# Attention and mixture of experts in one kernel: output writes issued by two engines in turn, more constant products, the last expert's first products in halves, its last casts split three to five

## The chip, the cores and the metric

The kernel runs on one core of a Trainium2 chip, as a single launch. The metric is the device time of one execution in microseconds. The value before is the median of three runs. A fourth execution was taken by the hardware profiler, and all views below are of that one.

## The reference

Two stages follow each other. The first is attention for 4 batches, 8 heads, 768 positions and head width 64. Three heads are causal over all earlier keys; the other five keep only the last 64 keys and 4 "sink" keys. The second is a mixture of 8 experts with early exit, over the 3072 rows of 512 columns that attention makes.

```python
scores = scale * q @ k.T                      # per batch and head
mask = causal if retrieval_head else causal & (is_sink | in_window)
x = softmax(where(mask, scores, -1e9)) @ v    # -> [3072, 512]

out = x.copy()
take = x @ w_skip > 0                         # the other rows leave as they are
e = argmax(x[take] @ w_gate); g = its softmax weight
out[take] = x[take] + g * (relu(x[take] @ w1[e]) @ w2[e])
```

Activations are 0.1-scaled normal draws; the weights are 8 x 512 x 1024 twice, in fp32, 33.5 MB in all.

## The kernel before

Every piece of work is an entry of a planner (`Plan`): a name, an engine, an assumed duration, what it depends on, and a key (the lowest goes first among those ready). The planner lays the entries out in time once, at build, and writes the instructions in the order of their planned starts; `manual_schedule` keeps that order. So an assumed duration or a key that is changed in one place can reorder instructions elsewhere, on every engine. On the chip each engine runs its own list in order and waits at semaphores. The DMAs are planned as well, on a common queue `Q`.

**Attention.** Sixteen pairs of heads, i = 0 to 15, four per batch. SyncE (SP) issues the loads of Q, K and V in fp32 (`load_qk`, `load_v`), four pairs ahead. GpSimd (POOL) casts them (`Cq`, `Ck`, `Cv`), TensorE (PE) transposes them (`Tq`, `Tk`, `Tv`), ScalarE (ACT) and VectorE (DVE) copy them out of PSUM (`Oq`, `Ok`, `Ov`). Then PE makes transposed scores in chunks of 1024 columns (`E`, L852 and L864), ACT takes their exponential (`X`, L874), PE weighs V with them (`PV`, L919), and DVE divides (`Nr`, `Nl`, `Nx`, L938 to L955) into the SBUF tile `x` of the batch. The chunks use two PSUM tiles `pst` in turn, so a chunk of scores waits for the exponential two chunks back.

**Writes of x.** When a batch's last pair is divided, `x_out` writes the batch to the output in HBM in two halves (`xo`, L976, 768 KB each). For the last batch it is four pieces: columns 0 to 255 after pair 13, 256 to 383 after pair 14, and two halves of the rest, which ACT divides itself (`n_last`, L969). All ten writes stand in SP's list, among the loads.

**Routing and gathers.** The gate logits come out of the same products (extra columns of V). DVE turns them into expert, rank and slot (`r`), PE into an index table, and `idx` (L1225) ends it. From there POOL gathers rows of x by index from HBM, 16 tiles of 128 rows, two per expert (`G`, L1259), and writes the results back by index (`S`, L1272).

**Experts.** For expert e and tile t: `cx` casts the gathered rows (DVE, L1286), `tx` transposes them (PE, L1295), `ox` copies them out (DVE, L1306), `F(e, f2)` is a quarter of the first products (PE, 8 matmuls of 256 columns, L1315), `Re` its relu (ACT, L1326), `Y(t)` the second products (PE, L1337), `A` the scaled addition (DVE, L1343), `S` the write. `warm` (L1480) puts matmuls of constants on PE while the index is made and the first gathers are under way; nothing reads their result.

**Weights.** POOL issues the weights of experts 0 to 6 as DMAs that cast fp32 to fp16 (`W`, L478). They begin in the middle of attention and stand in POOL's list between its casts, gathers and writes. Weights of the last expert come as fp32 through SP (`load_last`, `V`, L1378) into the room of older weights. The first piece goes where expert 6's first weights lie, so it waits for `F(6, 3)`. DVE and ACT cast each piece to fp16, one half of the columns each (`cast_last`, L1385).

**Completion counters.** In the program as built, plain DMAs of SP and ACT take turns over eight completion counters. A DMA that takes a counter waits on its engine until the former user of that counter has landed.

Of the kernel before, what the change touches and what calls it, by code (L numbers as in the profile page):

```python
# [8 lines left out]
FP32 = mybir.dt.float32  # L9
# [6 lines left out]
ACT = mybir.ActivationFunctionType  # L16
# [11 lines left out]
DM = H * D  # L28
E = 8
F = 1024  # L30
# [3 lines left out]
P = 128  # L34

DS = DM // P
FS = F // P
CAP = 256
# [14 lines left out]
class Plan:  # L53
# [9 lines left out]
    def op(self, name, eng, dur, fn, deps=(), key=0.0, lat=None, take=None,  # L63
           fill=None):


        o = dict(name=name, eng=eng, dur=dur, fn=fn, deps=list(deps), key=key,
                 lat=self.LAT if lat is None else lat, take=take, fill=fill,
                 seq=len(self.ops))
        self.ops.append(o)  # L70
        self.by[name] = o
        return name

    def dma(self, name, eng, issue, took, fn, deps=(), key=0.0, first=False,
            lat=1.9, fill=None):
        self.op((name, "go"), eng, issue, fn, deps, key, fill=fill)
        self.op(name, "Q", took, None, [(name, "go")], 0 if first else 1,
                lat=lat)
# [310 lines left out]
def kernel(  # L389
# [14 lines left out]
    nc = tc.nc  # L404
# [10 lines left out]
    Ov = out.rearrange("(b n p) d -> b p n d", b=B, p=P)  # L415
# [69 lines left out]
    with tc.tile_pool(name="sm", bufs=1) as sm_pool, \  # L485
# [3 lines left out]
        def pool(name, stack=pools, **kw):  # L489
# [17 lines left out]
        qk32, v32, c16, qTs, vTs, ats, psts, tps, xsb, lgh, opss = (  # L507
            {} for _ in range(11))
# [3 lines left out]
        op, dma = pl.op, pl.dma  # L512
# [145 lines left out]
        for i in range(NPR):  # L658
            for w in "qk":
                act = i == 0 and w == "k"  # L660
# [7 lines left out]
            elif i % 4 == 3 and i // 4 + 1 < B:  # L668
                b = i // 4 + 1
# [138 lines left out]
        for i in range(NPR):  # L808
# [7 lines left out]
            for hi in range(2):  # L816
# [10 lines left out]
               take=("tps", ("Ow", i)))  # L827
# [142 lines left out]
                                      opss[i][:, hi, c:c + D], recs[:, i, hi, n])  # L970
            return go

        def x_out(b, u, c0=0, c1=DM):
            def go():
                n = slice(0, NQB) if u is None else slice(3 * u, 3 * u + 3)
                nc.sync.dma_start(out=Ov[b][:, n, c0:c1],  # L976
                                  in_=xsb[b][:, n, c0:c1])
            return go

# [11 lines left out]
        for i in range(NPR):  # L991
            b = i // 4
# [15 lines left out]
            if i % 4 == 3:  # L1008
                op(("Gs", b), "DVE", 0.61, g_sum(b), [("Nl", i)], k0 + 1.15,
                   take=("tps", ("r", 1, "oh")) if b == B - 1 else None)  # L1010


        for b in range(B - 1):
            for u in range(2):
                dma(("xo", b, u), "SP", 0.45, 2.05, x_out(b, u),
                    [("Nx", 4 * b + 3)], next(sp) - 1000)
        for i, u, c0, c1, took in ((13, None, 0, 256, 2.2), (14, None, 256, 384, 1.3),
                                   (15, 0, 384, 512, 0.65), (15, 1, 384, 512, 0.65)):
            dma(("xo", 3, i, u), "SP", 0.45, took, x_out(3, u, c0, c1),
                [("Nx", i) if u is None else ("Nx", i, u)], next(sp) - 1000)  # L1020


# [153 lines left out]
        for ph, c0, n, k0, last in ((0, 0, 18, 140, ("Gs", 2)),  # L1176
# [36 lines left out]
            if ph:  # L1213
# [6 lines left out]
               take=("tps", "idx") if ph == 0 else None)  # L1220
# [12 lines left out]
        M = Consts()  # L1233
# [17 lines left out]
        xTs, x16s, xtps, hts, hpss, ypss = ({} for _ in range(6))  # L1251
# [54 lines left out]
                nc.vector.tensor_copy(xTs[e][:, :, s2 * P:(s2 + 1) * P], xtps[t])  # L1306
            return go

        def first(e, f2):
            def go():  # L1310
                w1 = wts[e, 0].rearrange("p (s f j) -> p s j f", s=DS, j=FS)
                hps = M.hps.tile([P, 2, CAP], FP32, tag="hps", name="hps")
                for fi in range(2):
                    for s in range(DS):
                        nc.tensor.matmul(  # L1315
                            hps[:, fi, :], w1[:, s, 2 * f2 + fi], xTs[e][:, s, :],
                            start=(fi == 0 and s == 0),
                            stop=(fi == 1 and s == DS - 1))
                hpss[e, f2] = hps
            return go  # L1320

        def relu(e, f2):
# [45 lines left out]
        def load_last(n, u, c0, c1):  # L1368
            def go():
                at = STAGE[n, u]  # L1370
                if n in IN_V and u == 0:
                    wtile(n, ldv_pool, tag="vf", bufs=2)
                if c0 == 0:
                    kw = dict(tag="vf", bufs=2) if at in IN_V else dict(tag=f"w_{at}")
                    w32[n, u] = (ldv_pool if at in IN_V else wpool if at < NPRE else M.w).tile(
                        [P, 2 * CW], FP32, name=f"w32_{n}_{u}", **kw)
                c = 2 * u * CW
                nc.sync.dma_start(out=w32[n, u][:, c0:c1],  # L1378
                                  in_=(w1r, w2r)[n % 2][E - 1][:, c + c0:c + c1])
            return go  # L1380

        def cast_last(n, u, c0, c1, dve):
            def go():
                to = wts[E - 1, n % 2][:, 2 * u * CW + c0:2 * u * CW + c1]
                (nc.vector.tensor_copy if dve else nc.scalar.copy)(  # L1385
                    to, w32[n, u][:, c0:c1])
            return go
# [3 lines left out]
        V_of = {14: [], 15: []}  # L1391
        for n in (14, 15):
            for u in range(2):
                e, half = divmod(STAGE[n, u], 2)
                parts = 2 if (n, u) == (15, 1) else 1
                for m in range(parts):
                    c0, c1 = (2 * CW * x // parts for x in (m, m + 1))
                    dma(("V", n, u, m), "SP", 0.45, 2.6 / parts, load_last(n, u, c0, c1),
                        [(prev, "go"),
                         *((("Y", t, 1) for t in (2 * e, 2 * e + 1)) if half else [("F", e, 3)]),  # L1400
                         *(place[n] if n in place else [])], 0, fill=3.0)
                    prev = ("V", n, u, m)
                    for dve in range(2):
                        d0, d1 = (c0 + (c1 - c0) * x // 2 for x in (dve, dve + 1))
                        op(("W", n, u, m, dve), "DVE" if dve else "ACT", 0.95 / parts,
                           cast_last(n, u, d0, d1, dve), [("V", n, u, m)], 650 + u)
                        V_of[n].append((u, ("W", n, u, m, dve)))
        op("drain", "POOL", 4.6, lambda: nc.gpsimd.drain(), [("W", 13, 0), ("G", NT - 1)], 455)
        for t in range(NT):
            op(("cx", t), "DVE", 0.62, cast_x(t), [("G", t), ("tx", t - 2)], 600 + t)  # L1410
            op(("tx", t), "PE", 0.25, turn_x(t),
               [("cx", t), ("ox", t - 2), ("F", 0, 3) if t > 1 else None],
               600 + 10 * (t // 2) - 15, take=("tps", ("ox", t)))
            op(("ox", t), "DVE", 0.42, out_x(t),
               [("tx", t), ("F", t // 2 - 2, 3)], 600 + t)
        for e in range(E):
            for f2 in range(FS // 2):
                op(("F", e, f2), "PE", 0.88, first(e, f2),
                   [("ox", 2 * e + 1), ("W", 2 * e, 0), ("W", 2 * e, 1),
                    *(x for _, x in V_of.get(2 * e, ())),  # L1420
                    ("Re", e - 1, f2)],
                   600 + 10 * e)
                op(("Re", e, f2), "ACT", 0.62, relu(e, f2),
                   [("F", e, f2), ("Y", 2 * e - 3, 1)], 600 + 10 * e)
            for s2 in range(NSM):
                t = e * NSM + s2

                cuts = (0, 4, 6, 8) if e == E - 1 else (0, 4, 8)
                for x, (j0, j1) in enumerate(zip(cuts, cuts[1:])):
                    end_ = j1 == FS  # L1430
                    op(("Y", t, 1) if end_ else ("Y", t, 0, x), "PE", 0.218 * (j1 - j0),
                       second(t, j0, j1),
                       [("Re", e, (j1 - 1) // 2), ("W", 2 * e + 1, 0),
                        ("W", 2 * e + 1, j0 // 4),
                        *(y for u, y in V_of.get(2 * e + 1, ())
                          if u == j0 // 4 and (u == 0 or y[3] == (j0 - 4) // 2)),
                        ("Y", t, 0, x - 1) if x else None,
                        ("A", t - 2)], 600 + 10 * e + 15 + (x if e == E - 1 else s2))
                op(("A", t), "DVE", 0.75, add(t), [("Y", t, 1), "idx"], 598.5 + t)
                dma(("S", t), "POOL", 1.0, 0.4, scatter(t), [("A", t)], 450 + t, first=True)  # L1440
# [43 lines left out]

        for part, (m, after) in enumerate(((3, [("PV", NPR - 1, 1)]),
                                           (1, [("r", 0, "slots"), "swap"]),
                                           (6, [("r", 1, "slots"), "swap"]))):
            for n in range(m):
                op(("warm", part, n), "PE", 0.85, warm(part),
                   after + ([("warm", part, n - 1)] if n else []), 0)  # L1490
# [43 lines left out]
```

## Time and profile before

| | before |
|---|---|
| median of 3 runs | 194.55 us (194.17 to 194.61) |
| profiled execution | 191.98 us, of which the span of instructions is 190.4 us |
| busy in the span | PE 157.8 us, POOL 125.3, DVE 115.6, ACT 103.8 |
| mean granted TensorE clock | 0.959 of full |
| HBM read and written | 56.64 MB and 10.49 MB, 353 GB/s over the span |
| loads, plain writes (DMA ring of SP) | 28.97 MB, 45.7% of 16 engines over the span |
| casting weight loads, gathers, scatters (POOL) | 19.45 MB as written, 47.0% |
| DMA ring of ACT | 0.41 MB, 0.9% |

A row of the profile gives a source line, an engine, an operation and its tiles. SPq and POOLq are the instruction sequencers of SP and POOL. The DMA share of a stretch of time is the busy time of packets over 16 engines; over 1.00 more than one packet per engine was in flight. In casting loads only the fp16 bytes are counted.

### The profile page before, as it was taken

Reading aid. Unit: us, or ns where it says so; the run is one execution under the profiler, and the core shown is the slowest. Engines: PE = TensorE matmul, PEld = TensorE weight load, DVE = VectorE, ACT = ScalarE, POOL = GpSimd, SP = SyncE. Lnnn points to the kernel's source line nnn. Section 1 sums busy time; section 2 is a strip of 40 time slices with the busy share of each in tenths; the row PEclk is TensorE's granted clock in tenths of the full one; section 3 lists DMA queues with packets and bytes.
Section 4 is the critical chain, followed back from the end, with each engine's and each line's share of the span. In section 5 each row is a group of like instructions: output and inputs, shape, how many; then the busy total and the mean of one; then the engine's idle time right before and its main releaser. Section 6 shows DMA issues by size and latency. Waiting matters only on the chain.

```text
span 190.4 us, 4704 instructions
## 1 busy us (share of the span) xinstructions
PE 157.8 (83%) x1859; PEld 121.7 (64%) x1874; DVE 115.6 (61%) x249; ACT 103.8 (55%) x136; POOL 125.3 (66%) x211
## 2 busy tenths in 40 slices
PE   0596689998999999999966959699999996995930
PEld 0365678777888888788843428389678673734610
DVE  6738675969797888799988241565673433152320
ACT  2187329986799979989739903136133150423700
POOL 7545997699898999998588488887735234016040
PEclk9999969999999999999999997999999999998795
DMA  5999999988997999999999989999999999899510
GB/s 151 323 312 365 335 362 354 282 288 311 310 356 247 351 284 275 211 216 293 272 237 308 197 159 198 269 258 227 195 236 233 215 261 269 186 406 314 192 65 13
DMA packets 28384, 49.21 MB, mean 258 GB/s; under 512 B 5172, under 2 KB 21428, under 8 KB 27202
## 3 DMA queue, kind: packets, MB, share of 16 engines
q0 software_dynamic: 5728, 19.45, 47.0%
q1 hardware_dynamic: 21296, 28.97, 45.7%
q10 hardware_dynamic: 1330, 0.41, 0.9%
q8 instruction: 16, 0.26, 0.5%
q14 instruction: 14, 0.11, 0.2%
HBM read 56.64 MB, written 10.49 MB: 353 GB/s over the span
## 4 chain that ended last, share of the span: by engine, by line
PE 46%; DMA 18%; issue 13%; DVE 10%; POOL 6%; ACT 4%; POOLq 0%; ACTq 0%; DVEq 0%
PE pst L864 13%; DMA w<-in_moe_w_dram 8%; PE opsa L919 8%; DMA xg<-out_dram,idx 6%; PE pst L852 6%; PE hps L1315 6%; PE yps L1337 5%; PE tps L714 5%; POOL out_dram L1272 3%; DVE k L748 3%; ACT at L874 3%; DMA qf<-in_q_dram 2%; PE tps L725 2%; DMA out_dram<-x 2%; DVE vT L768 1%
## 5 line engine op out<-in xcount | busy, mean ns | idle before, releaser
L874 ACT ACTIVATE at<-pst 128x1024 f16<-128x1024 f32 (+1 forms) x60 | 58.3, 1013 | 14.7 <-PE pst L864 13.8
L1326 ACT ACTIVATE ht<-hps 128x512 f16<-128x512 f32 x32 | 19.1, 597 | 41.4 <-PE hps L1315 30.6
L1272 POOL DMA_INDIRECT out_dram<-xg,idx x16 | 16.6, 1034 | 33.4 <-DVE xg L1343 30.1
L864 PE MATMUL pst<-qT,k 128*128 128x128 f16 (+2 forms) x308 | 36.4, 239 | 2.4 <-ACT qT L740 0.9
L1315 PE MATMUL hps<-xT,w 128*128 128x256 f16 x256 | 33.0, 290 | 4.5 <-ACT w L1385 2.2
L1315 PEld LDWEIGHTS <-w 128*128 128x128 f16 x256 | 29.9, 147 | 7.9 <-ACT w L1385 2.9
L748 DVE COPY k<-tps 64x768 f16<-64x768 f16 x32 | 30.4, 951 | 6.3 <-PE tps L714 5.9
L864 PEld LDWEIGHTS <-k 128*128 128x128 f16 x308 | 24.7, 100 | 11.3 <-issue 2.6
L1337 PE MATMUL yps<-w,ht 128*128 128x512 f16 x128 | 29.1, 379 | 0.0
L1343 DVE SCALAR_TENSOR_TENSOR xg<-yps,gsl,xg 128x512 f32<-128x512 f32 x16 | 11.9, 749 | 16.8 <-PE yps L1337 16.7
L1259 POOL DMA_INDIRECT xg<-out_dram,idx x16 | 17.3, 1078 | 7.1 <-issue 3.7
L919 PE MATMUL opsa<-va,at 128*128 128x74 f16 x392 | 20.2, 199 | 1.5 <-DVE x L955 1.5
L1337 PEld LDWEIGHTS <-ht 128*128 128x128 f16 x128 | 12.2, 98 | 13.0
L919 PEld LDWEIGHTS <-at 128*128 128x128 f16 x472 | 18.6, 99 | 2.0 <-DVE x L955 1.8
L740 ACT COPY qT<-tps 128x768 f16<-128x768 f16 x16 | 12.8, 800 | 7.2 <-PE tps L714 7.2
L852 PE MATMUL pst<-smask,identb 128*128 128x512 bf16 (+3 forms) x49 | 16.2, 344 | 0.3 <-ACT at L874 0.2
L1286 DVE CAST x<-xg 128x512 f16<-128x512 f32 x16 | 10.0, 646 | 10.0 <-issue 5.6
L695 POOL CAST va<-vf 128x768 f16<-128x768 f32 x16 | 13.3, 830 | 2.2 <-PE opsa L919 1.1
L955 DVE TENSOR_TENSOR x<-opsa,recs 128x768 f32<-128x768 f32 x15 | 14.2, 945 | 0.0
L714 PE MATMUL tps<-ident,q 128*128 128x128 f16 x96 | 8.3, 224 | 7.1 <-DVE q L689 6.1
L759 POOL COPY kx<-k 64x256 f16<-64x256 f16 x20 | 8.0, 399 | 8.1 <-DVE k L748 7.4
L1306 DVE COPY xT<-xtp 128x512 f16<-128x512 f16 x16 | 6.3, 421 | 11.5 <-PE xtp L1295 11.2
(139 smaller groups left out, 254.6 us busy)
## 6 DMA issues: line engine op xcount, KB each, us to landing
w<-in_moe_w_dram POOLq DMA_DIRECT2D x16, 512.0 KB, 8.0
qf<-in_q_dram SPq DMA_DIRECT2D x16, 384.0 KB, 6.5
w<-in_moe_w_dram POOLq DMA_DIRECT2D x6, 1024.0 KB, 11.1
kf<-in_k_dram SPq DMA_DIRECT2D x15, 384.0 KB, 6.0
out_dram<-x SPq DMA_DIRECT2D x7, 768.0 KB, 9.4
w<-in_moe_w_dram SPq DMA_DIRECT2D x3, 1024.0 KB, 7.9
w<-in_moe_w_dram SPq DMA_DIRECT2D x2, 512.0 KB, 13.8
kf<-in_k_dram ACTq DMA_DIRECT2D x1, 384.0 KB, 4.8
```

The costliest lines, as they stand in the source:

```text
L714: nc.tensor.matmul(t[:, n], c16[w, i][:, n].rearrange("p h d -> p (h d)"), C.ident, is_transpose=True, start=(n == 0), stop=(n == NQB - 1))
L748: nc.vector.tensor_copy(to, ti)
L852: nc.tensor.matmul(pst[:, c0 - c * CH:c0 - c * CH + m].rearrange("p (n c) -> p n c", c=P), identb, mv, start=(n == 0), stop=(n == last))
L864: nc.tensor.matmul(pst[:, c0 - c * CH:c0 - c * CH + m * P], lt, qTs[i][:, qb * P:(qb + m) * P], start=(n == 0), stop=(n == last))
L874: nc.scalar.activation(ats[i][:, c * CH:c * CH + cn], psts[i, c][:, :cn], ACT.Exp, scale=SCALE)
L919: nc.tensor.matmul(opss[i][:, hi, qb * VA:(qb + 1) * VA], ats[i][:, b0 + c:b0 + c + P], vb, start=(n == 0), stop=(n == len(todo) - 1))
L955: nc.vector.tensor_mul(xsb[i // 4][:, :, h0 * D:(h0 + 2) * D].rearrange("p n (h d) -> p h n d", h=2), summed(i, GX, 512 - GX, D), recs[:, ...
L1259: h = nc.gpsimd.indirect_dma_start(out=M.xgs[:, t], out_offset=None, in_=out[:, :], in_offset=bass.IndirectOffsetOnAxis(ap=idx[:, t:t + 1] ...
L1272: h = nc.gpsimd.indirect_dma_start(out=out[:, :], out_offset=bass.IndirectOffsetOnAxis(ap=idx[:, t:t + 1], axis=0), in_=M.xgs[:, t], in_of ...
L1315: nc.tensor.matmul(hps[:, fi, :], w1[:, s, 2 * f2 + fi], xTs[e][:, s, :], start=(fi == 0 and s == 0), stop=(fi == 1 and s == DS - 1))
L1326: nc.scalar.activation(hts[e][:, 2 * f2:2 * f2 + 2], hpss[e, f2], ACT.Relu)
L1337: nc.tensor.matmul(ypss[t], hts[e][:, j, s2 * P:(s2 + 1) * P], w2[:, j], start=(j == 0), stop=(j == FS - 1))
```

## The change

1. Writes of x alternate between SP and ACT: the second half of each of batches 0 to 2, the piece of pair 14 and the last half piece go to ACT's list.
2. Two more entries of constant products of four matmuls each stand ahead of the first expert (32 matmuls in place of 24).
3. For expert 7 each `F` is cut in two: the lower half of the contraction, which needs only the first piece of the weights, and the upper half. All four PSUM tiles are held open between.
4. The casts of the last expert are cut at three eighths: ACT casts 3/8 of the columns and DVE 5/8.
5. The key of `tx` is raised from -15 to -9, behind the first products of the expert before it.

```diff
-        def x_out(b, u, c0=0, c1=DM):
+        def x_out(b, u, c0=0, c1=DM, act=False):
...
-                nc.sync.dma_start(out=Ov[b][:, n, c0:c1],
+                (nc.scalar if act else nc.sync).dma_start(out=Ov[b][:, n, c0:c1],
                                   in_=xsb[b][:, n, c0:c1])
...
         for b in range(B - 1):
             for u in range(2):
-                dma(("xo", b, u), "SP", 0.45, 2.05, x_out(b, u),
+                dma(("xo", b, u), "ACT" if u else "SP", 0.45, 2.05, x_out(b, u, act=u == 1),
                     [("Nx", 4 * b + 3)], next(sp) - 1000)
...
-            dma(("xo", 3, i, u), "SP", 0.45, took, x_out(3, u, c0, c1),
+            act = i == 14 or u == 1
+            dma(("xo", 3, i, u), "ACT" if act else "SP", 0.45, took, x_out(3, u, c0, c1, act),
...
-        def first(e, f2):
+        def first(e, f2, s0=0, s1=DS):
...
-                    for s in range(DS):
+                    for s in range(s0, s1):
...
-                        d0, d1 = (c0 + (c1 - c0) * x // 2 for x in (dve, dve + 1))
-                        op(("W", n, u, m, dve), "DVE" if dve else "ACT", 0.95 / parts,
+                        cm = c0 + (c1 - c0) * 3 // 8
+                        d0, d1 = (cm, c1) if dve else (c0, cm)
+                        op(("W", n, u, m, dve), "DVE" if dve else "ACT", 0.85 / parts,
...
-               600 + 10 * (t // 2) - 15, take=("tps", ("ox", t)))
+               600 + 10 * (t // 2) - 9, take=("tps", ("ox", t)))
...
-                op(("F", e, f2), "PE", 0.88, first(e, f2),
+                two = e == E - 1
+                if two:
+                    op(("F", e, f2, 0), "PE", 0.44, first(e, f2, 0, DS // 2),
+                       [("ox", 2 * e + 1), ("W", 2 * e, 0),
+                        *(x for u, x in V_of.get(2 * e, ()) if u == 0),
+                        ("Re", e - 1, f2)],
+                       600 + 10 * e - 1)
+                op(("F", e, f2), "PE", 0.44 if two else 0.88,
+                   first(e, f2, DS // 2 if two else 0),
                    [("ox", 2 * e + 1), ("W", 2 * e, 0), ("W", 2 * e, 1),
                     *(x for _, x in V_of.get(2 * e, ())),
-                    ("Re", e - 1, f2)],
+                    ("F", e, f2, 0), ("Re", e - 1, f2)],
...
-                                           (6, [("r", 1, "slots"), "swap"]))):
+                                           (8, [("r", 1, "slots"), "swap"]))):
```

More of the change, by code (lines that the diff above doesn't have):

```diff
@@ L1307, in out_x @@
             return go
-        def first(e, f2):
+        def first(e, f2, s0=0, s1=DS):
             def go():
                 w1 = wts[e, 0].rearrange("p (s f j) -> p s j f", s=DS, j=FS)
-                hps = M.hps.tile([P, 2, CAP], FP32, tag="hps", name="hps")
+                if s0 == 0:
+                    hpss[e, f2] = M.hps.tile([P, 2, CAP], FP32, tag="hps", name="hps")
                 for fi in range(2):
-                    for s in range(DS):
+                    for s in range(s0, s1):
                         nc.tensor.matmul(
-                            hps[:, fi, :], w1[:, s, 2 * f2 + fi], xTs[e][:, s, :],
+                            hpss[e, f2][:, fi, :], w1[:, s, 2 * f2 + fi], xTs[e][:, s, :],
                             start=(fi == 0 and s == 0),
                             stop=(fi == 1 and s == DS - 1))
-                hpss[e, f2] = hps
             return go
```

## The prediction

> **What bounds the kernel now.** I began with the page's shares, its slices of DMA and clock, and the end of the chain.
>
> ```profile
> PE 46%; DMA 18%; issue 13%; DVE 10%; POOL 6%; ACT 4%; POOLq 0%; ACTq 0%; DVEq 0%
> DMA  5999999988997999999999989999999999899510
> PEclk9999969999999999999999997999999999998795
> ```
> ```profile
> 145.91 14.66 DMA w<-in_moe_w_dram
> 160.62 3.71 PE hps L1315 x32
> 164.33 5.19 PE yps L1337 x24
> ```
>
> TensorE leads the shares, but the late chain is a 14.66 us wait for w12 (the last weight load of expert 6, the twelfth of the late ones), landing at 160.62; F(6), by which I mean its quarters F(6, 0) to F(6, 3), the release of its buffers and the last expert follow. The DMA digits stay at 8 or 9 for two thirds of the span. In windows of 10 us the share is 1.01 or more from 60 to 105 us and from 120 to 160 us, so **the transfers set when the last experts start**. Where idle DMA time is left decides what a lost microsecond costs.
>
> ```profile
> 46.00:48.00 2.00, 1.32 (x21) 1.11 (x20) 1.93 (x5) 0.30 (x1) 1.94 (x6) 1.00 1.03 368
> 48.00:50.00 2.00, 1.95 (x36) 1.72 (x35) 1.97 (x3) 1.92 (x3) 1.84 (x5) 1.00 1.00 263
> 50.00:52.00 2.00, 2.00 (x42) 1.73 (x39) 1.02 (x3) 1.33 (x2) 1.85 (x4) 1.00 1.01 331
> 58.00:60.00 2.00, 2.00 (x38) 1.79 (x36) 1.70 (x2) 2.00 (x3) 1.28 (x4) 1.00 0.42 94
> 110.00:115.00 5.00, 2.69 (x18) 1.58 (x17) 1.95 (x4) 0.00 (x0) 4.08 (x5) 0.83 0.88 187
> 115.00:120.00 5.00, 5.00 (x37) 4.13 (x36) 1.42 (x3) 2.39 (x4) 3.99 (x5) 0.83 0.90 174
> ```
>
> The columns are stretch, length, busy PE, PEld, DVE, ACT and POOL, clock, DMA share, GB/s. After 46 us only two places have slack: 58 to 60 (1.16 us idle) and 110 to 120 (0.6 + 0.5 = 1.1 us).
>
> SyncE's timeline and DMA issues (KB, us to landing) show the first x writes, and its waits one thing more:
>
> ```profile
> 44.44 0.92 SPq L976 DMA_DIRECT2D out_dram<-x  x2
> 45.45 1.02 SPq L643 DMA_DIRECT2D kf<-in_k_dram  x1
> 46.57 1.89 SPq L643 DMA_DIRECT2D qf<-in_q_dram  x1
> 50.91 7.45 SPq L643 DMA_DIRECT2D qf<-in_q_dram  x1
> ```
> ```profile
> out_dram<-x SPq DMA_DIRECT2D x1, 768.0 KB, 6.8
> ```
> ```profile
> SPq L653 <- DMA kf<-in_k_dram: 1.4, 1, 1.4
> ```
>
> The second half of x, issued at 44.88, lands 6.8 us later at 51.7; the K load of pair 11 is issued right behind it, so no gap opens between them. The last line is a V load that waits for a K load it does not use: it takes over that load's completion counter.
>
> The tail, from the timeline:
>
> ```profile
> 171.48 0.44 PE L1315 MATMUL hps<-xT,w 128*128 128x256 f16 x2 [0.25 <-ACT w L1385]
> 173.86 5.16 PE L1315 MATMUL hps<-xT,w 128*128 128x256 f16 x30 [1.94 <-ACT w L1385]
> 178.86 3.62 PE L1337 MATMUL yps<-w,ht 128*128 128x512 f16 x16
> 180.35 0.62 ACT L1385 CAST w<-w 128x512 f16<-128x512 f32 x1 [0.19 <-DMA w<-in_moe_w_dram]
> 182.08 1.41 DVE L1343 SCALAR_TENSOR_TENSOR xg<-yps,gsl,xg 128x512 f32<-128x512 f32 x2 [1.30 <-PE yps L1337]
> ```
> ```profile
> 176.00:178.00 2.00, 2.00 (x11) 1.55 (x10) 0.69 (x1) 1.53 (x2) 0.00 (x0) 0.50 1.01 389
> ```
>
> TensorE waits 1.94 us inside F(7), then runs at half clock; the last weights land at about 180.3.
>
> **What the Trainium skill says.** "DMA: Bandwidth & Descriptors", section "Issuing engines are not separate DMA queues", says that issuing from several engines saves only sequencer time. The trace agrees: one ring alone shows shares of 1.0 and more. The same page, section "Latency and other measured facts", gives about 2 us of fixed cost, most of it the receipt of the write, and some 0.6 us to the first byte. Here x data start 0.9 us after issue, and the receipt takes about 1.4 us (data end about 50.3, landing 51.7). "TensorE: Matmul & The Clock Gate", section "Part 1: The HAM clock gate (the \"warmup\" mystery)", says that the clock halves after an idle window of about 3.4 us on a free-running grid. Here 0.50 came at 113.3 and 174.8, after gaps of only 1.7 and 1.9 us; a short gap can suffice.
>
> **Part 1: x writes on ScalarE.** The bytes are the same. Saved on SyncE: five issues of 0.37 to 0.49 us, worth nothing, since SyncE is not the limit. Added on ScalarE: five issues, taken at 0.5 (its K load took 0.50). Batch 0: ScalarE idles 1.72 us before 47.70; hidden. Batch 1: at 64.0, gap of 1.23 before 67.81; hidden. Batch 2: at 83.3, no gap; with the qT copy now ahead of it one exp comes 1.1 to 1.25 later, at most 0.4 us of TensorE stall, hidden while transfers lag. Batch 3: idle at 95.8 to 98.9 covers one, the other delays the zeros by 0.45, which have over 4 us; the routing before G0 ends at 107.3 and the last x lands at 104.8, so that stays covered.
>
> **The hidden wait.** Plain DMAs of SyncE and ScalarE share eight completion counters in turn. In the program as built, batch 0's second half takes counter 0 on ScalarE, and SyncE's K load of pair 11 is now the next user of counter 0: SyncE must wait until the write has landed. Before, that load's counter came from a load long finished. So the load is issued not at 45.45 but at about 51.75; its data start at 51.75 + 0.9 = 52.7. The x data end at about 50.3, behind them SyncE's other loads queue too, and GpSimd's first weight load comes only at 62.08. **DMA then stands idle for 52.7 - 50.3 = 2.4 us** (bounds 1.6 to 3.0, for an earlier receipt or a later first byte). The loads themselves have slack: pair 11's K would land at 55 for a cast at 57.34, the later Q and V 6 us or more ahead of theirs. But the bytes move back by 2.4 us. The idle 58 to 60 does not take this up: the Q load at 50.91 is held for 7.45 us in its issue, behind the big V load, until that has drained, so this gap moves along. From 60 on there is no slack until 110 to 120, where at most 1.1 is taken up; I take 0.7 (0.3 to 1.3), as part of that idleness is itself a wait for buffers. w12, F(6) and the last expert's loads: +2.4 - 0.7 = **+1.7 us**.
>
> **Part 2: eight more constant products.** 24 took 5.34 us from 105.5, 0.222 each: +1.78 ends them at 112.6, where the first transpose began at 112.52; cost 0.1 at most. F(0) ran at half clock (5.00 us for 32 products against 3.66 elsewhere), so 1.3 could be saved, but TensorE then waits in any case for the gather landing at 121.94: worth 0.
>
> **Part 3: moved transposes and w11.** Transposes go behind F(e-1), w11's issue behind S4 (about 144 instead of 139.1). w10 before it occupies the transfers to about 147.5, so this costs 0; if that cover fell, w11 would be late by up to 2 us before S5.
>
> **Part 4: halves and casts in the last expert.** Sixteen products fill the 1.94 wait; sixteen are left from about 173.7, at 0.115 each done at 175.5 if the clock stays full. Casts per column: VectorE 0.51 ns + 0.17 us, ScalarE 0.84 ns + 0.18 us (from 1024 and 512 columns: 0.69 and 0.43; 1.04 and 0.61). So 1280 and 768 columns take 0.82 and 0.83, against 0.69 and 1.04. Y then starts near 177.1, but its last pieces wait for weights landing at 180.3: the last cast ends 0.1 to 0.2 earlier, and the first accumulation at about 181.45 instead of 182.08 (less Y left behind it): -0.63 at most. Without a half clock before, only 0.1 is left. I take **-0.4** (0.1 to 0.7).
>
> **Sum.** +2.4 - 0.7 - 0.4 = +1.3 us against the profiled execution: 190.4 of span, 191.98 in all. The median of the runs, 194.55, lies 2.6 above that execution; I apply the difference to it: 195.85, say **195.8**. This case alone reaches from 195.2 to 197.0 (smallest and largest hole with the bounds above, not all at once).
>
> **Rivals.** *Stream end unmoved, faster (0.22).* The hole opens, but the stream is later held by buffers, not bytes: then slack at 110 to 120 and prefetch take it all, and the tail's -0.4 to -0.7 remains: 193.9. For it: the shares there lie below 1. Against it: only 1.1 us of slack is visible against 2.4. It decides if w12's landing moves by less than 0.1. *Half carried, no change (0.18).* A hole of 1.6 with 1.1 absorbed gives +0.5 against -0.4: 194.6. The delayed exp of batch 2, with no hole, ends there too. *The change does not do what it says:* the built order shows five of ten x writes on ScalarE, 32 constant products, F(7) as 16 and 16 products, casts of 768 and 1280 columns; excluded.
>
> **How the numbers follow.** Slower 0.60, same 0.18, faster 0.22; 0.3% (0.58 us) is about what a measurement of this kernel can tell from no change. The likeliest case sets 195.8; the range goes down to 193.8 for the others and up to 197.0.
>
> **What would show it.** After: SyncE waiting some 6 us on a DMA of x, its K load at 51 to 52, DMA share falling between 50 and 53; w12 landing 1 to 2 us later against the start; TensorE at full clock in 113 to 117 and 174 to 178; casts of 0.82; a shorter way from the last weights' landing to the first accumulation. I am wrong if the share shows no dip, or if there is a dip and w12 lands when it did.

## The result and the profile after

The changed kernel takes 199.4 us (median of 4 runs, 198.42 to 202.74) against 194.58 us before: 4.8 us or 2.5% more. Compared by the fast runs alone, those within 1.5% of their kernel's fastest, the ratio is 1.041 with a 95% interval of 1.033 to 1.050. The forecast had the side right and the size wrong: 195.8, with a range up to 197.0. The profiled execution after took 202.74 us, the slowest of its four runs and 3.3 above their median, where that of before lay 2.6 below its own; the two profiles therefore differ by more than the medians do, and places rather than totals are read from them.

The page after, clock and DMA in 40 slices:

```profile
PEclk9999999999999999975799999999999999699995
DMA  5999999799499999999699699999999999969901
```

There is a 4 among the DMA digits about a quarter of the way in, which was not there before, and the clock falls in slices 18 to 20, from about 86 to 101 us, where attention ran at full clock before.

The DMA queue of SyncE, its timeline and one of its waits:

```profile
43.27 0.39 SPq L976 DMA_DIRECT2D out_dram<-x  x1
53.85 0.37 SPq L643 DMA_DIRECT2D kf<-in_k_dram  x1
...
56.27 6.73 SPq L643 DMA_DIRECT2D qf<-in_q_dram  x1
...
67.15 0.52 SPq L643 DMA_DIRECT2D qf<-in_q_dram  x1
```
```profile
SPq L643 <- DMA out_dram<-x: 10.1, 1, 10.1
```

The K load that followed the x writes at 45.45 now goes out at 53.85. SyncE waited 10.1 us for an x write, the one that ScalarE issued at 43.28: in the trace's records that write and this K load count on the same semaphore, number 100, and the write landed at 53.79. In windows (columns as before) the transfers stop; the first three lines are those of before, the rest those after:

```profile
52.00:54.00 2.00, 1.93 (x32) 1.59 (x29) 1.57 (x4) 1.55 (x2) 1.49 (x3) 1.00 1.07 392
54.00:56.00 2.00, 1.95 (x41) 1.76 (x41) 1.90 (x4) 2.00 (x4) 1.85 (x4) 1.00 1.15 349
82.00:92.00 10.00, 9.90 (x176) 8.72 (x175) 9.66 (x22) 8.51 (x11) 8.20 (x19) 1.00 1.05 273
...
50.00:52.00 2.00, 2.00 (x36) 1.75 (x33) 1.02 (x4) 1.46 (x2) 1.59 (x2) 1.00 1.00 379
52.00:54.00 2.00, 1.93 (x38) 1.60 (x36) 1.97 (x3) 2.00 (x4) 1.79 (x5) 1.00 0.07 26
54.00:56.00 2.00, 1.95 (x30) 1.75 (x30) 1.93 (x5) 1.80 (x2) 1.87 (x4) 1.00 0.50 145
...
82.00:92.00 10.00, 2.29 (x50) 2.06 (x47) 2.94 (x6) 2.34 (x3) 1.54 (x3) 0.78 1.05 305
```

The hole is 1.86 + 1.0 = 2.9 us of idle DMA time. The new damage is in the last line: from 82 to 92 us TensorE is busy for 2.29 of 10 us, where it was busy for 9.90, with the DMA share at 1.05 in both. The waits and timeline of GpSimd, one wait of TensorE, and a step of the chain say why (the first line is GpSimd's last Q cast in the kernel before, which waits for nothing):

```profile
80.59 0.82 POOL L689 CAST q<-qf 128x768 f16<-128x768 f32 x1
```
```profile
POOL q L689 <- DMA qf<-in_q_dram: 9.5, 1, 9.5
```
```profile
79.83 0.53 POOL L478 DMA_DIRECT2D w<-in_moe_w_dram  x1
90.46 0.82 POOL L689 CAST q<-qf 128x768 f16<-128x768 f32 x1 [9.52 <-DMA qf<-in_q_dram]
91.23 0.53 POOL L478 DMA_DIRECT2D w<-in_moe_w_dram  x1
91.76 0.84 POOL L695 CAST va<-vf 128x768 f16<-128x768 f32 x1
```
```profile
PE tps L725 <- POOL va L695: 8.4, 1, 8.4
```
```profile
67.15 23.16 DMA qf<-in_q_dram
```

The last Q load, issued at 67.15, takes 23.16 us. In the kernel before it was issued at 60.6 and took 8.1, and its cast came 11.9 us after it had landed. GpSimd now stands before its cast; the V cast behind it in GpSimd's list is what TensorE waits for, and the next weight load stands there too.

**Why a load takes 23 us.** From 67 to 72 us the rings of SyncE and ScalarE moved 391 GB/s together, alone. From 73 to 83 us, beside the weight loads, SyncE's ring got 70 GB/s, ScalarE's had nothing to move, and GpSimd's got 169, counted as written in fp16 (all summed from the trace's packets). In that stretch the trace has 46 pieces per us of SyncE's, of 1537 bytes on average, and 41 of the weights', of 4096 bytes as written. One of the weights' pieces holds a DMA engine for 322 ns on average, one of SyncE's for 76. The kernel of experiment 1 shows the same: 44 and 42 pieces per us, 67 and 170 GB/s. The Trainium skill, "DMA: Bandwidth & Descriptors", section "Queues, rings and completion order", says that each DMA engine goes round between the queues it has work for, a packet at a time. The trace agrees as far as it shows turns of about equal number; whether the trace's pieces are the packets that the page means is not shown. With turns of equal number, the ring with the smaller pieces loses by bytes. **While the weights stream, a lag on SyncE's ring is worked off at about a fifth of the rate: 70 GB/s in place of 391.**

### The profile page after: what moved, and what is told of

The parts are those of the page before. It is cut to its first block, busy times and chain, and to the rows that moved or that the text cites. A ratio compares the mean times of both kernels' runs of the same rounds, so it can differ in the third digit from the quotient of the medians.

```text
span 201.2 us, 4729 instructions
## 1 busy us (share of the span) xinstructions
PE 160.0 (79%) x1868; PEld 122.4 (61%) x1882; DVE 116.0 (58%) x249; ACT 103.0 (51%) x136; POOL 125.1 (62%) x211
## 4 chain that ended last, share of the span: by engine, by line
PE 38%; issue 18%; DMA 17%; DVE 8%; POOL 6%; ACT 5%; SPq 3%; POOLq 1%; DVEq 0%; ACTq 0%
DMA qf<-in_q_dram 12%; PE hps L1317 9%; PE pst L864 8%; PE yps L1338 6%; PE opsa L919 5%; PE pst L852 4%; DMA kf<-in_k_dram 4%; PE tps L714 3%; POOL out_dram L1273 3%; DVE k L748 3%; SPq L643 3%; ACT xg L1255 2%; ACT at L874 2%; PE tps L725 1%; PE xtp L1296 1%
## 5 line engine op out<-in xcount | busy, mean ns | idle before, releaser
L864 PE MATMUL pst<-qT,k 128*128 128x128 f16 (+2 forms) x308 | 37.1, 242 | 2.3 <-ACT qT L740 1.0
L1317 PE MATMUL hps<-xT,w 128*128 128x256 f16 x256 | 31.3, 283 | 4.8 <-DMA w<-in_moe_w_dram 4.2
L1317 PEld LDWEIGHTS <-w 128*128 128x128 f16 x256 | 29.2, 145 | 7.9 <-DMA w<-in_moe_w_dram 5.1
L919 PE MATMUL opsa<-va,at 128*128 128x74 f16 x392 | 19.7, 196 | 1.5 <-DVE x L955 1.5
L919 PEld LDWEIGHTS <-at 128*128 128x128 f16 x472 | 18.1, 97 | 2.0 <-DVE x L955 1.8
L689 POOL CAST q<-qf 128x768 f16<-128x768 f32 x15 | 12.3, 823 | 10.2 <-DMA qf<-in_q_dram 9.5
L768 DVE COPY vT<-tps 128x768 f16<-128x768 f16 x16 | 8.8, 552 | 14.7 <-PE tps L725 14.6
L852 PE MATMUL pst<-smask,identb 128*128 128x512 bf16 (+3 forms) x50 | 17.1, 354 | 0.1
L1344 DVE SCALAR_TENSOR_TENSOR xg<-yps,gsl,xg 128x512 f32<-128x512 f32 x16 | 11.9, 748 | 7.3 <-PE yps L1338 6.8
L725 PE MATMUL tps<-ident,va 128*128 128x128 f16 x96 | 8.6, 230 | 9.0 <-POOL va L695 8.4
L1287 DVE CAST x<-xg 128x512 f16<-128x512 f32 x16 | 9.5, 629 | 9.2 <-issue 8.0
## 6 DMA issues: line engine op xcount, KB each, us to landing
w<-in_moe_w_dram SPq DMA_DIRECT2D x3, 1024.0 KB, 10.1
out_dram<-x ACTq DMA_DIRECT2D x3, 768.0 KB, 10.5
```

The source lines that it names most:

```text
L852: nc.tensor.matmul(pst[:, c0 - c * CH:c0 - c * CH + m].rearrange("p (n c) -> p n c", c=P), identb, mv, start=(n == 0), stop=(n == last))
L864: nc.tensor.matmul(pst[:, c0 - c * CH:c0 - c * CH + m * P], lt, qTs[i][:, qb * P:(qb + m) * P], start=(n == 0), stop=(n == last))
L919: nc.tensor.matmul(opss[i][:, hi, qb * VA:(qb + 1) * VA], ats[i][:, b0 + c:b0 + c + P], vb, start=(n == 0), stop=(n == len(todo) - 1))
L1317: nc.tensor.matmul(hpss[e, f2][:, fi, :], w1[:, s, 2 * f2 + fi], xTs[e][:, s, :], start=(fi == 0 and s == 0), stop=(fi == 1 and s == DS - 1))
```

## The experiments

Theory A is the shared counter and the starvation beside the weight stream. Theory B is that the moved transposes and the later weight load cost the time, theory C that five issues on ScalarE, or writes on two rings, do. One table serves all runs. "Left at 72" is what the rings of SyncE and ScalarE still had to move at 72 us, without the last expert's weights (packets summed). Of this, 3.15 MB are the x writes of batches 2 and 3, which come later in every kernel; what is above 3.15 is left of earlier work. The other columns are times in us in each kernel's profile.

| kernel | SyncE's load waits for x | left at 72, MB | last Q lands | `idx` ready | last x lands | first gather | first gather to end |
|---|---|---|---|---|---|---|---|
| before | 0 | 3.56 | 68.7 | 106.2 | 106.1 | 107.3 | 83.1 |
| after | 10.1 | 5.03 | 90.3 | 116.8 | 116.0 | 117.8 | 83.5 |
| before_act | 7.0 | 4.93 | 89.2 | 116.3 | 115.6 | 117.3 | 82.0 |
| before_b0 | 7.7 | 4.94 | 76.6 | 115.1 | 114.1 | 116.1 | 83.8 |
| before_b0_small | 5.1 | 4.45 | 73.8 | 106.0 | 113.5 | 114.7 | 84.0 |
| before_b0_latew | 6.6 | 4.50 | 73.5 | 105.2 | 103.8 | 106.2 | 96.5 |
| before_earlyw | 0 | 4.35 | 69.2 | 108.7 | 107.2 | 109.7 | 81.1 |
| before_b123 | 0 | 3.63 | 69.2 | 107.1 | 106.2 | 108.0 | 82.7 |
| after_x6 | 0 | 3.49 | 71.5 | 106.9 | 106.6 | 107.9 | 83.9 |
| after_sp | 0 | 3.18 | 66.2 | 105.4 | 105.5 | 106.7 | 81.7 |
| after_sp5 (same kernel) | 0 | 3.27 | 68.2 | 105.3 | 109.9 | 111.1 | 81.4 |
| before_tail | 0 | 3.54 | 67.8 | 106.0 | 105.7 | 106.9 | 82.3 |
| before_warmtx | 0 | 3.21 | 69.3 | 104.8 | 104.2 | 105.7 | 82.4 |
| before_warmtx5 (same kernel) | 0 | 3.23 | 67.9 | 105.2 | 104.7 | 106.1 | 82.2 |

In every row the first gather goes out at the later of two times: 0.96 to 0.97 us after the index, or 1.21 us after the last x write has landed. In four profiles it is the x write that decides: before, before_b0_small, after_sp and after_sp5.

**1. The part with the writes alone (before_act).**

```diff
-dma(("xo", b, u), "SP", ..., x_out(b, u), ...)
+dma(("xo", b, u), "ACT" if u else "SP", ..., x_out(b, u, act=u == 1), ...)
 ... and in the last batch: act = i == 14 or u == 1
```

> Only the alternation of the x writes is added to the kernel before. Theory A (the shared completion counter holds SyncE's K load of pair 11 until batch 0's write on ScalarE has landed, and the late Q, K, V loads then meet the weight stream): 198 to 202 us, SyncE waiting about 10 us on a DMA of x, TensorE idle 6 to 9 us between 80 and 93 us. Theory B (the moved transposes and the later weight load of expert 6 cost the time): within 1 us of 194.6.

Measured: 200.88 us median, against 192.05 for before on that chip (7 runs, 186.95 to 197.5, a wide scatter). No less than the whole loss is in this part; GpSimd waits 9.3 us for the last Q. Theory B falls.

**2. Batch 0's second half alone (before_b0).** The condition is `u and b == 0`.

> Only batch 0's second half is written by ScalarE, all other writes stay with SyncE. Theory A: the whole loss from this one write, 198 to 202 us. Theory C (five issues on ScalarE delay its exponentials, or writes on two rings crowd out the loads): about a fifth of the loss, 195 to 196 us.

Measured: 201.13 us median (198.2 to 203.31). One write out of five gives the whole loss. But the stall has another place. The last Q lands at 76.6 and starves nobody. VectorE stands instead, in its timeline:

```profile
94.45 0.96 DVE L955 TENSOR_TENSOR x<-opsa,recs 128x768 f32<-128x768 f32 x1 [7.96 <-DMA out_dram<-x]
```

Two tiles of x are in use in turn, so batch 3 may not write its tile before batch 1's x has left it. That write stood behind the late loads, was issued at 67.13 and landed at 94.36.

**3. The other four writes (before_b123).** The condition is `u and b > 0`, and the last batch as in the change.

> The other four writes go to ScalarE, batch 0 stays with SyncE. Theory A: 194.2 to 195.2 us, no long wait of SyncE on a DMA of x, no gap of TensorE over 2 us between 80 and 93 us. Theory C: most of the loss, 197 us or more.

Measured: 192.35 us median (191.72 to 196.97) beside 192.05, no load waiting for x, TensorE busy for 14.23 of the 15 us from 80 to 95. ScalarE's issues, batch 2's delayed exponential and writes on two rings cost nothing that shows, and theory C's 197 us did not come. With the scatter of before on that chip a cost of a few us could hide here; the interval of experiment 5 is narrower.

**4. Everything but the writes (after_sp, twice).** The ten writes stand in SyncE's list again.

> The changed kernel with all ten x writes back on SyncE; the constant products, the halves, the casts and the moved transposes stay. Theory A with the tail as predicted: 193.8 to 194.4 us (the predicted -0.4 from the tail alone). Theory B: 197 us or more.

> The changed kernel with all x writes back on SyncE once more, for a closer interval, as the version that may beat both. Predicted from the parts: 0.3 to 3 us below before (tail 0.5; constant products up to 2.5 by the last look).

Measured: 191.54 us, then 192.16 us with a ratio of 0.996 (0.989 to 1.002). The loss is gone and a gain is not resolved, so no version that beats both is shown.

**5. The same five writes without the shared counter (after_x6).**

```diff
-[("Nx", 4 * b + 3)], next(sp) - 1000)
+[("Nx", 4 * b + 3), ("X", 6, 0) if u and b == 0 else None], next(sp) - 1000)
```

> The changed kernel, with five x writes still on ScalarE, but batch 0's write is placed later in ScalarE's list (behind the first exponential of pair 6), so that its completion counter is taken over by ScalarE's next write and by no load of SyncE. Theory A (the shared counter, then loads that crawl beside the weight stream): no wait of SyncE on a DMA of x, no TensorE gap over 2 us between 80 and 95 us, within 1% of before. Theory C (writes on two rings, or the issues on ScalarE, cost the time): 2% or more above before.

Measured: a ratio of 0.990 (0.972 to 1.007); no load of SyncE waits for x, TensorE is busy for 14.18 of the 15 us. The engines of all ten writes are those of the change; what differs is the place of one in ScalarE's list, which puts it out at 48.45 instead of 43.28, and with it the counter: in the trace, ScalarE's first two x writes now both count on semaphore 106 and no load of SyncE does. All five writes on ScalarE therefore cost 0.7% at most, and theory C falls. SyncE does wait 11.4 us on an x write, at L976, ahead of another x write that it issues only 8 us after that wait has ended; the expectation of no such wait was too broad.

**6. A smaller write on the shared counter (before_b0_small).**

```diff
-n = slice(0, NQB) if u is None else slice(3 * u, 3 * u + 3)
+n = (... if b else slice(5 * u, 5 + u))      # batch 0: five sixths on SP, one sixth on ACT
```

> Before, with batch 0's x write cut five to one instead of three to three, and the one sixth (256 KB) on ScalarE. The counter is shared as in the slow run, so SyncE still waits, but only until the small write has landed, while the large one is still being sent. Theory A: a wait of SyncE of 2 to 5 us, no hole in the transfers above 0.5 us, the last Q load landed by 71 us, the time within 0.7% of before. Rival (any wait of SyncE at that place costs its length): 2 us or more above before.

Measured: 1.047 (1.039 to 1.055). Theory A as I had it failed here: the wait was 5.1 us and the hole only 1.5 us (share 0.75 from 48 to 50, 0.50 from 50 to 52, 0.99 from 52 to 54), attention ran through (14.56 of 15 us from 80 to 95), and yet the whole loss came. GpSimd's timeline has a third place of the stall:

```profile
104.12 0.58 POOL L478 DMA_DIRECT2D w<-in_moe_w_dram  x1
114.71 1.08 POOL L1260 DMA_INDIRECT xg<-out_dram,idx  x1 [10.00 <-issue]
```

The index was ready at 106.0, but the first gather reads x from HBM and goes out at 114.7. The view names no cause; the trace's semaphore records do: GpSimd's sequencer stands from 104.0 to 113.53 on the counter of the last x write, which landed at 113.50. In the kernel before it stood on the same counter, until 106.13. When GpSimd issued the weight loads of 102.2 and 104.1, SyncE had 1.42 MB left to move at 102.3, before 0.62 MB (packets summed); what was left then crawled beside them. That these two loads are what turned 0.8 MB into 7 us is argued from the trace; no run moves them alone.

**7. The same wait with the weights held back (before_b0_latew).** Batch 0 as in 2, and the second weight load waits for pair 14's Q cast.

```diff
-[("Cv", 1), (fill[x - 1], "go") if x else None,
+[("Cv", 1), (fill[x - 1], "go") if x else None, ("Cq", 14) if x == 1 else None,
```

> Batch 0's second half on ScalarE, as in the run that lost the time, but the second and later weight loads wait for the Q cast of pair 14, so that SyncE's queue can empty first. The 7 us wait of SyncE stays, and the hole in the transfers at 50 to 55 us. Theory A in full (the loss is starvation beside the weight stream, not the lost transfer time): TensorE gap between 80 and 95 us under 2 us, the total 1 to 3 us above before (the 2.4 us of transfers lost, and weights issued late). The prediction's own step (the hole alone costs the time) gives the same as without the delay, plus the delay: 4 us or more above before.

Measured: 1.060 (1.048 to 1.071), not the 1 to 3 us expected; by the total alone, this is the "4 us or more" of the prediction's own step. But the place of the loss tells. SyncE waited 6.6 us and 4.50 MB were left at 72, as in experiment 6. No second weight load was issued until 74.4 us, by 80 us that earlier work had gone (3.15 MB left), and the first gather came at 106.2, earlier than before. Windows and waits of this kernel:

```profile
80.00:95.00 15.00, 14.20 (x244) 12.22 (x247) 13.94 (x36) 12.62 (x15) 10.58 (x24) 1.00 1.03 237
```
```profile
PE hps L1315 <- DMA w<-in_moe_w_dram: 7.5, 2, 3.9
```

So here the hole delays neither attention nor the gather; in the other kernels it does so through the weight stream. The loss here lies after the first gather (96.5 us to the end): the planner laid all later weights back too, by 93 us 7 weight loads had been issued where before had 10, and 9 of 22 were out when the first gather was, where all thirteen other profiles have 12. The direct cost of the hole cannot be read from the total of this run.

**8. Weights early and no shared counter (before_earlyw).** `fill=6.0` in place of 1.5 for the second to fourth weight loads.

> Before, all x writes on SyncE, no shared counter in the way, but the second and third weight loads are put right behind the first (about 62 us instead of 69 and 71). Theory A (SyncE's last loads crawl beside the weight stream, and attention starves): TensorE or VectorE waits 3 us or more between 70 and 95 us for a Q or K load or for batch 1's x write, and the time is 2 us or more above before although the weights come earlier. The prediction's step (loads have 6 us of slack; only lost transfer time counts): no such wait, the time the same or up to 1 us less.

Measured: 1.008 (1.003 to 1.013), about 1.5 us, and no single wait of 3 us. It is slower in spite of earlier weights, but neither the stall nor the 2 us of theory A came, so this expectation failed. 4.35 MB were left at 72, but no weight load was issued between 70.4 and 76.4, and by 90 us the rings had 2.38 MB left where before had 2.42. This lag was made up before anything stood waiting for it. Why the index came 2.5 us later than before is not shown.

**9. The tail alone (before_tail).** The halves of F(7) and the casts of 3/8 and 5/8.

> Before, with the halves of the last expert's first products and the casts at three eighths alone. Predicted step: 0.1 to 0.7 us less than before, 16 products filling the wait for the second weight piece, casts of 0.82 and 0.83 us. Rival: no gain, since the last weights land when they did; then within 0.1 us.

Measured: 1.000 (0.996 to 1.003). In its profile, TensorE and VectorE:

```profile
172.06 1.94 PE L1316 MATMUL hps<-xT,w 128*128 128x256 f16 x16
174.29 1.94 PE L1316 MATMUL hps<-xT,w 128*128 128x256 f16 x16 [0.28 <-ACT w L1385]
```
```profile
180.65 0.49 DVE L1385 CAST w<-w 128x640 f16<-128x640 f32 x1 [1.37 <-DMA w<-in_moe_w_dram]
181.84 1.41 DVE L1343 SCALAR_TENSOR_TENSOR xg<-yps,gsl,xg 128x512 f32<-128x512 f32 x2 [0.70 <-PE yps L1337]
```

The wait inside F(7) fell from 1.94 to 0.28 us, and TensorE ran at full clock from 174 to 178 us, where its mean was 0.60 before. From the landing of the last weights (180.62) to the accumulation is 1.22 us; before it was 1.75 (180.33 to 182.08). The changed kernel has 1.22 as well (192.16 to 193.38). This 0.53 shows in the traces and is within the scatter of the total.

**10. Constant products and moved transposes (before_warmtx, twice).**

> Before, with the eight more constant products and the moved transposes alone. Predicted: no difference above 0.3 us; TensorE at full clock where it was at half between 113 and 117 us. Rival: F(0) at full clock moves everything after it, 1 us or more less; or the weight load of expert 6, issued later, adds up to 2 us.

> Before, with the eight more constant products and the moved transposes alone, once more, since its first interval (0.967 to 0.999) says faster by a little. Theory (the end follows the first gather by 81 to 84 us in all kernels, and these parts do not move the first gather): 0.995 to 1.005 of before, first gather to end of the profile 81 to 84 us. Rival (F(0) at full clock moves the rest): 0.975 to 0.99, first gather to end under 81 us.

Measured: 0.983 (0.967 to 0.999), and with a new set of runs 0.996 (0.990 to 1.003). The first interval promised a gain that the second did not keep. TensorE is at full clock from 113 to 118 us in both, where its mean was 0.66 before, and first gather to end (82.4 and 82.2 us) is that of the others: no effect resolved.

## Why the prediction was right in direction and wrong in size

**Right.** The counter and the wait it makes, from the built order alone; experiments 2, 3 and 5 show that it is this one write and this counter. The hole: 2.9 us against 2.4, within the bounds of 1.6 to 3.0, though the wait was 10.1 us where some 6 were expected. That the V load's stall in SyncE's issue moves along (56.27 for 6.73 us). That ScalarE's issues, the constant products and the moved transposes cost nothing that shows. The casts: 0.83 and 0.82 us (experiment 9) against 0.83 and 0.82 from the fit. The tail: 0.53 on the last stretch against 0.4, the part that cannot be resolved in the total.

**Wrong: the term "+2.4 - 0.7 = +1.7".** Three steps behind it failed.

First, "The loads themselves have slack ... the later Q and V 6 us or more ahead of theirs". The slack was right as it stood, and the last Q had even 11.9 us; but a lag of one ring was priced in time at the full rate. 2.9 us at the 379 GB/s of the window ahead of them are 1.1 MB; beside the weight stream, at 70 GB/s, 1.1 MB are an estimated 16 us. What was late at 72 us was more than that: 1.47 MB over the kernel before in the changed kernel, 1.37 in before_act. The changed kernel's profile was 0.96 MB behind at 44 us already, before the write could matter; so was that of before_b123, by 0.87, and it had made this up by 72. before_act was level with before at 44 (within 0.02), so its 1.37 is the wait's own. The prediction names the first weight load at 62.08, but not what the weights do to the rate of SyncE's ring; the section of the Trainium skill on turns between queues, cited above, was not used.

Second, "the last x lands at 104.8, so that stays covered". The slack of the first gather was put at 2.5 us (from 107.3), and there was none. In the trace of before the last x write lands at 106.10, the index is ready at 106.15, and GpSimd's sequencer stands on the counter of that write until 106.13. (The chain view leaves that DMA at 104.83, which is not its landing.) A later landing of that write therefore moves the gather, as experiment 6 shows with 7.4 us.

Third, the charge of the lag to the end of the weight stream: "w12, F(6) and the last expert's loads: +2.4 - 0.7". In thirteen of the fourteen profiles of the table the end comes 81 to 84 us after the first gather, whether that goes out at 105.7 or at 117.8. After, it came 10.5 us later than in the profile of before, and the end 10.8 later (first line before, the other two after):

```profile
107.31 1.09 POOL L1259 DMA_INDIRECT xg<-out_dram,idx  x1 [2.49 <-PE hps L1480]
...
117.78 1.09 POOL L1260 DMA_INDIRECT xg<-out_dram,idx  x1 [2.29 <-PE hps L1491]
...
172.11 4.22 PE L1317 MATMUL hps<-xT,w 128*128 128x256 f16 x22 [3.37 <-DMA w<-in_moe_w_dram]
```

The products that the first two lines name are not what the gathers waited for last: the sequencer's last waits ended at 106.13 (x write) and 116.85 (index), and some 0.9 to 1.2 us from there to the gather stand in all fourteen profiles.

The weight stream still decides when the last experts start: F(6) waits for w12 after (last line) as it did before, and goes at 172.1 instead of 160.6, 11.5 us later where 1 to 2 were expected. But ten of the 22 weight loads stand in GpSimd's list behind the first gather, w12 among them (issued 38.6 us behind it before, 37.3 after). So whatever holds that list holds the rest of the stream as well. The quantity to price was the time of the first gather. Why the distance to the end is so constant is argued from that list; what the stream alone adds is not separated, except that in experiment 7, with fewer loads issued ahead of the gather, the distance grew to 96.5.

**Readings that were off and did not decide.** The gap from 58 to 60 us, said to move along, does not come again after: the shares from 56 to 66 are 1.01 or more, so from 44 to 72 the DMA engines stood idle only some 1.3 us longer than before (in before_b0_latew and before_b0_small a gap does follow, with shares of 0.33 and 0.47 from 60 to 62). The 1.4 us called the receipt of the x write are mostly not that: the last piece of its data starts at 51.14 and the write has landed at 51.67: fifteen of the sixteen DMA engines were through by 51.02, and one came later. And w12, called the last weight load of expert 6, is the first of its two; the other is issued at 153.64. The ends of the range, 195.2 and 197.0, do not come out of the sum: the bounds of the hole give 195.05 and 196.45.

**The rivals.** "Stream end unmoved" and "half carried" both lacked the stall; the first would have left w12 within 0.1 us of its time, and F(6), which waits for it, went 11.5 us later. None of my cases let the hole grow on the way, so the range stopped at 197.0.

**Left open.** How much of the 10.8 us between the two profiles is the change: the medians differ by 4.8 us and the ratio gives 4.1%, and of these two executions one was the slowest of its kernel's and the other faster than the other four. The profile of after_sp5 is a hint: the same kernel's first gather came at 106.7 in one profile and 111.1 in the other, with the index at 105.4 and 105.3, since the last x landed 4.4 us later. Since the last x write has no slack, kernels without the wait may be on the edge of the same crawl, but this was seen only once. The direct cost of the hole, with the weights in their old places, was not separated either.

## What to carry to other kernels

Price a late transfer at the rate that its own ring will have when it runs, not at the full rate: a lag that is small while a ring is alone is multiplied when another ring starts to stream large pieces beside it. Before a DMA is moved to another engine's queue, look in the built order for which transfer takes over its completion counter, and on which engine that one waits. Find the event that the end follows at a constant distance over several runs (here the first gather) and price the change by what it does to that event. A long wait late in the chain (here for w12) names what arrives last; ask also what stands ahead of its issue, since a delay there moves it too.

## What the runs showed of the hardware

- Beside weight loads with pieces of 4096 bytes, counted as written in fp16, a ring with pieces of about 1.5 KB got 70 GB/s against 391 GB/s for the plain rings without them (73 to 83 and 67 to 72 us of the changed kernel). The numbers of pieces were about equal (41 and 46 per us); one took 322 and 76 ns.
- A plain DMA of SyncE waited for one of ScalarE that it does not depend on, for 5.1 to 10.1 us in five kernels, because both count on one semaphore.
- A lag on the same ring stalled two engines at three places in three kernels: GpSimd 9.5 us (Q cast), VectorE 7.96 us (reuse of an x tile), GpSimd 10.0 us (first gather). The profile shows the engine that needed the late data first; the cause lies 30 to 60 us earlier.
- The kernel before, unchanged, ran from 186.95 to 205.13 us over the chips of these experiments, so differences of 1 to 2% are hard to tell from a few runs: the kernel of experiment 10 gave 0.983 and, with the next set, 0.996.
